# First threshold search of the second MoE layer: next thresholds prepared beside the count, list in three parts, and the second expert's rows turned later

## The chip, the cores and the metric

The kernel runs on one core of a Trainium2 chip. The metric is device time in microseconds (us) of one execution, as a median of several. Engines are named as the profile names them: PE is TensorE (matmuls; PEld its weight loads), DVE is VectorE, ACT is ScalarE, POOL is GpSimd, SP is SyncE, which here issues DMAs. Every engine runs its own instructions strictly in the order in which the program gives them to it; semaphores tie the engines together.

## The reference

Attention over local windows and block summaries gives x of 3072 tokens by 512. A first MoE layer (each token to its best expert) gives a new x. The second MoE layer, where the change is, gives every expert exactly `cap` tokens:

```python
def _moe2_ref(x, w_gate, w1, w2):
    N, D = x.shape; E = w_gate.shape[1]       # 3072, 512, 8
    cap = N // E                              # 384
    logits = x @ w_gate
    order = np.argsort(-logits.flatten())
    assigned = -np.ones(N); counts = np.zeros(E)
    for idx in order:                         # best (token, expert) pair first
        tok, e = idx // E, idx % E
        if assigned[tok] >= 0 or counts[e] >= cap: continue
        assigned[tok] = e; counts[e] += 1
    out = np.zeros((N, D))
    for e in range(E):                        # F = 1024
        mask = assigned == e
        out[mask] = np.maximum(x[mask] @ w1[e], 0.0) @ w2[e]
    return out
```

All data is float32. The results must be near float32, so each operand of a large product is split in two parts, high and low (`wh`, `wl`; `dxh`, `dxl`; `dhh`, `dhl`), and three matmuls stand for one.

## The kernel before

**Stages.** `phase_a` does the attention (to about 178 us), `phase_b` the first experts and the logits of the second layer, left in `Lm` (to about 324 us), `phase_d` the second experts with the routing that `Route2` computes.

**Routing.** The greedy assignment is done in eight phases. Phase `ph` finds the next expert that fills up: a search of NSTEP = 5 steps, each with 31 thresholds, for the logit value at which some expert has `cap` candidates. One step is a chain: thresholds `p_thr` from the step's lower bound (L792, `th` holds the bound `lo`), compares of all tokens' best logits with them (`p_g`, L797), 24 matmuls that count per expert (L806 in phase 0), a comparison with the room that is left (`p_sat`, L816, which also gives the flags `p_any`), a matmul that sums the flags over partitions (L829), and from that the new `lo` (L830). After the search the tokens of this expert are known (`p_t`, L851, summed by matmuls at L859 and L860; positions at L868). `list(ph)` makes a list of their numbers: one-hot matrices `l_A`, `l_bh`, `l_bv` (L888 to L893), matmuls into `dx_ps` (L899, later phases L902), and the index `p_ix` (L909).

**Constants.** `st_ps` is one PSUM tile that holds the small state of the search. `init_state` copies four constants there at the start of phase 0. The reduction into `v` (L778), the first step of a phase, writes to the same tile.

**Experts.** For each expert POOL gathers its 384 rows by three indirect DMAs (L943, tile `xg`), PE transposes them (`xT`, L954, three times four), ACT and DVE split them into `dxh` and `dxl` (L957). L1 is 32 steps of three matmuls (L965, L966, L967), after every fourth of which ACT and DVE make `dhh` (L970) and `dhl` (L972). L2 is 24 steps of three matmuls (L979, L980, L981); after every eighth ACT copies `dz` and POOL scatters it to the output (L986). Weights come by DMA (`wraw`), ACT casts the high part (L927), POOL subtracts for the low part (L936, the function `lows`).

**What sets the order.** From phase 0's list on, a planner in `phase_d` decides while the program is built. It keeps clocks of its own (`now[0]` for PE, `dve`, `pool`), adds an assumed duration for every step that it places, and puts the parts of the next routing phase, the list, the gather, the casts and the transposes between the steps of L1 and L2 as soon as its clock says that they are ready. `xts_step` places the transposes of the next expert at the earliest 4.5 us after the gather by that clock:

```python
if q<=7 and xts.get(q,3)<3 and now[0]>=gath_t[q]+4.5+1.0*xts[q] and (cur is None or npc>=34+4*xts[q]):
```

A change of one of these numbers moves `now[0]`, and with it the place of everything that comes later.

## Time and profile before

| | us |
|---|---|
| median of three runs | 679.68 (677.44 to 681.78) |
| the profiled execution | 682.45 |
| its span in the trace | 680.8 |
| attention and first experts | 0 to 324 |
| search 0, list, gather, transposes | 324.8 to 360.2 |
| second experts, L1 of expert 0 to the last matmul | 360.2 to 675.4 |

The span is the time from the first to the last instruction; 1.65 us of the execution lie outside. A time given in the rows is the distance from the start of the span. In a row of the timeline the brackets at the end say how long the engine was idle before it and what ended that; xN means that N like instructions in a row are taken together. Matmul rows overlap: what counts is the distance of their starts.

### The profile page before, as it was taken

How to read it: one execution, taken by the hardware profiler on the slowest of the kernel's cores; microseconds unless marked ns; L12 is line 12 of the kernel's file. 1: busy time of each engine (PE TensorE's matmuls, PEld its weight loads, DVE VectorE, ACT ScalarE, POOL GpSimd, SP SyncE). 2: the span in 40 equal slices, each digit the busy share in tenths (PEclk: the TensorE clock that was granted, in tenths of full speed). 3: DMA queues.
4: the chain of work that ended last, by engine and by line, in shares of the span. 5: the costliest groups of instructions: out<-in, count | busy, mean ns of one | idle time of the engine just before them, and what ended most of it. 6: DMA issues, size and time to landing. Idle time of an engine off the chain costs nothing.

```text
span 680.8 us, 12765 instructions
## 1 busy us (share of the span) xinstructions
PE 612.7 (90%) x4427; PEld 501.7 (74%) x4427; DVE 487.7 (72%) x1866; ACT 318.4 (47%) x680; POOL 369.6 (54%) x400
## 2 busy tenths in 40 slices
PE   7878975999889999999448999999999999999996
PEld 5667765788567777776327878888897978879895
DVE  5686994889777889683775768788888888862120
ACT  5556873676743856761015135162433526154521
POOL 4322343352146289873027269394876939399841
PEclk8788997899789999998558999999999999999999
DMA  9999899976615987720035072553626154385201
GB/s 239 241 237 240 218 274 192 256 175 200 239 62 187 362 266 224 255 85 23 2 98 197 32 233 79 170 172 123 202 85 209 64 189 153 139 256 182 105 1 46
DMA packets 59778, 114.22 MB, mean 168 GB/s; under 512 B 13537, under 2 KB 23521, under 8 KB 58944
## 3 DMA queue, kind: packets, MB, share of 16 engines
q1 hardware_dynamic: 49968, 79.37, 40.1%
q0 software_dynamic: 9744, 34.02, 15.2%
q8 instruction: 35, 0.57, 0.4%
q14 instruction: 31, 0.25, 0.1%
HBM read 96.54 MB, written 14.88 MB: 164 GB/s over the span
## 4 chain that ended last, share of the span: by engine, by line
PE 22%; issue 10%; POOL 8%; DVE 6%; DMA 4%; ACT 1%; POOLq 0%; DVEq 0%
POOL wl L936 6%; PE dh_ps L965 4%; PE dh_ps L966 4%; PE dh_ps L967 4%; DMA xg<-xrows,p_ix 3%; PE dz_ps L979 2%; PE dz_ps L981 2%; PE dz_ps L980 2%; POOL out_dram L986 1%; PE rt_ps L810 1%; DMA wraw<-in_w1b_dram 1%; DVE p_g L797 1%; PE dh_ps L954 1%; PE rt_ps L806 0%; ACT wh L927 0%
## 5 line engine op out<-in xcount | busy, mean ns | idle before, releaser
L936 POOL TENSOR_TENSOR wl<-wraw,wh 128x512 fp32r<-128x512 f32 x124 | 155.6, 1296 | 5.1 <-ACT wh L927 4.7
L965 PE MATMUL dh_ps<-dxh,wh 128*128 128x384 f32 x256 | 90.0, 351 | 0.7 <-ACT dxh L957 0.7
L927 ACT CAST wh<-wraw 128x512 fp32r<-128x512 f32 x128 | 73.7, 620 | 35.9 <-DMA wraw<-in_w1b_dram 34.1
L966 PE MATMUL dh_ps<-dxl,wh 128*128 128x384 f32 x256 | 87.2, 341 | 0.5 <-DVE dxl L957 0.5
L967 PE MATMUL dh_ps<-dxh,wl 128*128 128x384 f32 x256 | 86.8, 339 | 0.0
L118 POOL TENSOR_TENSOR wraw<-wraw 96x512 f32<-96x512 f32 (+4 forms) x39 | 39.6, 1016 | 80.3 <-DMA wraw<-in_v_dram 77.9
L979 PE MATMUL dz_ps<-wh,dhh 128*128 128x512 f32 x192 | 79.1, 412 | 0.0
L981 PE MATMUL dz_ps<-wh,dhl 128*128 128x512 f32 x192 | 75.9, 395 | 0.0
L980 PE MATMUL dz_ps<-wl,dhh 128*128 128x512 f32 x192 | 75.9, 395 | 0.0
L972 DVE SCALAR_TENSOR_TENSOR dhl<-dh_ps,dhh 128x384 fp32r<-128x384 f32 x64 | 35.1, 555 | 49.0 <-ACT dhh L970 48.6
L986 POOL DMA_INDIRECT out_dram<-dz,io x24 | 24.3, 1014 | 81.3 <-ACT dz L984 78.5
L970 ACT ACTIVATE dhh<-dh_ps 128x384 fp32r<-128x384 f32 x64 | 31.4, 491 | 75.3 <-PE dh_ps L967 75.3
L984 ACT COPY dz<-dz_ps 128x512 f32<-128x512 f32 x24 | 14.1, 586 | 102.8 <-PE dz_ps L981 56.8
L138 ACT ACTIVATE p_e<-s_sb,nm 128x118 f32<-128x118 f32 x192 | 59.7, 385 | 0.9 <-DVE nm L132 0.9
L504 POOL TENSOR_TENSOR wl<-wraw,wh 128x1024 fp32r<-128x1024 f32 (+1 forms) x18 | 38.1, 2144 | 28.3 <-ACT wh L503 28.3
L503 ACT CAST wh<-wraw 128x1024 fp32r<-128x1024 f32 (+1 forms) x56 | 48.9, 932 | 8.0 <-DMA wraw<-in_w1a_dram 6.1
L943 POOL DMA_INDIRECT xg<-xrows,p_ix x24 | 23.4, 974 | 52.2 <-DVE rrow L875 32.5
L128 PE MATMUL s_ps<-kt,Q 128*128 128x118 f32 x192 | 42.5, 306 | 9.3 <-DVE kt L108 6.7
L965 PEld LDWEIGHTS dh_ps<-dxh,wh 128*128 128x128 f32 x256 | 48.8, 190 | 1.5 <-ACT dxh L957 0.9
L966 PEld LDWEIGHTS dh_ps<-dxl,wh 128*128 128x128 f32 x256 | 48.7, 190 | 1.3 <-DVE dxl L957 1.1
L967 PEld LDWEIGHTS dh_ps<-dxh,wl 128*128 128x128 f32 x256 | 48.7, 190 | 0.0
L504 DVE TENSOR_TENSOR wl<-wraw,wh 128x1024 fp32r<-128x1024 f32 (+1 forms) x38 | 42.7, 1163 | 8.0 <-ACT wh L503 8.0
(355 smaller groups left out, 1476.9 us busy)
## 6 DMA issues: line engine op xcount, KB each, us to landing
wraw<-in_w1b_dram SPq DMA_DIRECT2D x15, 1024.0 KB
wraw<-in_w2b_dram POOLq DMA_DIRECT2D x14, 1024.0 KB, 7.4
wraw<-in_w2a_dram SPq DMA_DIRECT2D x12, 1024.0 KB
wraw<-in_w1a_dram SPq DMA_DIRECT2D x10, 1024.0 KB
VV<-in_v_dram SPq DMA_DIRECT2D x16, 585.0 KB
kt<-in_k_dram SPq DMA_DIRECT2D x16, 412.0 KB
qd<-in_q_dram SPq DMA_DIRECT2D x16, 384.0 KB
wraw<-in_v_dram SPq DMA_DIRECT2D x8, 768.0 KB
```

The source lines that it names most:

```text
L128: T.matmul(p[:,j,0:118],d['q2'][:,h,w,:],d['k2'][:,h,w//2,:] if w%2 else d['kt'][:,h,64*w:64*w+118],start=True,stop=True)
L138: A.activation(pe[:,j,:],sb[:,j,:],AF.Exp,bias=nm[:,j:j+1],scale=-1.0)
L503: (hi.tensor_copy if hi else nc.scalar.copy)(h[:,c],t[:,c])
L504: (lo or nc.vector).tensor_tensor(l[:,c],t[:,c],h[:,c].bitcast(F32),op=OP.subtract)
L927: A.copy(h[:,c],t[:,c])
L936: eng.tensor_tensor(l[:,c],t[:,c],h[:,c].bitcast(F32),op=OP.subtract)
L965: T.matmul(q,wh[:,c],s['xh'][:,d,:],start=(d==0),stop=False)
L966: T.matmul(q,wh[:,c],s['xl'][:,d,:],start=False,stop=False)
L967: T.matmul(q,wl[:,c],s['xh'][:,d,:],start=False,stop=(d==3))
L979: T.matmul(q,s['hh'][:,f,c0],wh[:,c],start=(f==0),stop=False)
L980: T.matmul(q,s['hh'][:,f,c0],wl[:,c],start=False,stop=False)
L981: T.matmul(q,s['hl'][:,f,c0],wh[:,c],start=False,stop=(f==7))
```

## The change

1. `init_state` copies the four constants with ACT, all at the start of phase 0; before, DVE did two ahead of L778 and two in step 0, behind the compares. The addition that completes `Lm` is moved behind the two instructions that make `pm`.
2. In phase 0, the thresholds of steps 1 to 4 are made from the count directly: `pre` (the threshold numbers times the next width, plus the old lower bound) is computed after `p_sat`, and one SCALAR_TENSOR_TENSOR adds the count times the width. The new `lo` is computed behind the compares. The count's matmul writes `dx_ps` instead of `rt_ps`.
3. In phase 0's list, `l_A` is laid out with the weights of a matmul contiguous, is written last, and in three parts.
4. In the planner, the transposes of expert 1 are placed at the earliest 6.0 us after its gather by the planner's clock; 4.5 for the others as before.

```diff
--- before.py
+++ after.py
@@ -723,10 +723,10 @@
         for j in range(4): WC[k,j]=W.split(RAW[j],G if j==3 else None)
         xT(k); L1(k,0); L1(k,1); hT(k); L2(k); yT(k); place(k,pfc,cfc); direct(k); put(k)
         G.indirect_dma_start(out=xr,out_offset=bass.IndirectOffsetOnAxis(ap=gcol[:,1:2],axis=0),in_=YR[k],in_offset=None,bounds_check=128+N-1,oob_is_err=False)
-    Lm=st['Lm'].rearrange("p e c->p (e c)"); V.tensor_tensor(Lm,Lm,lgp[:,0:192],op=OP.add)
 
     V.tensor_reduce(st['pm'],st['pmx'],AX.X,OP.max)
     V.tensor_scalar(st['pm'].bitcast(U32),st['pm'].bitcast(U32),0x7F800000,None,op0=OP.bitwise_and)
+    Lm=st['Lm'].rearrange("p e c->p (e c)"); V.tensor_tensor(Lm,Lm,lgp[:,0:192],op=OP.add)
 
 NSTEP=5; J=31; BIG=1e30
 
@@ -752,11 +752,8 @@
     def state(self,nm,dt=None):
         return self.q[nm].bitcast(dt) if dt else self.q[nm]
     def init_state(self):
-        V=self.nc.vector; st=self.st
-        for nm,src in (('c8',st['c8']),('jr',self.jr)): V.tensor_copy(self.q[nm],src)
-        yield
-        for nm,src in (('colid',st['colid']),('p0',self.p0)): V.tensor_copy(self.q[nm],src)
-        yield
+        A=self.nc.scalar; st=self.st
+        for nm,src in (('c8',st['c8']),('jr',self.jr),('colid',st['colid']),('p0',self.p0)): A.copy(self.q[nm],src)
     def wide(self,ph): return 2 if ph<3 else 4
     def psum(self):
         return self.ps.tile([128,512],F32,name="rt_ps",bufs=1)
@@ -773,8 +770,8 @@
 
         nc,st,wk=self.nc,self.st,self.wk; V=nc.vector; T=nc.tensor
         B3=[128,8,24]; B4=[128,2,8,24]; Lm=self.Lm; c8=st['c8']
-        ini=self.init() if ph==0 else iter(()); inq=self.init_state() if ph==0 else iter(()); Q=self.state
-        next(inq,None)
+        ini=self.init() if ph==0 else iter(()); Q=self.state
+        if ph==0: self.init_state()
         v=Q('v'); V.tensor_reduce(v,Lm.rearrange("p e c->p c e"),AX.X,OP.max)
         if ph: yield 0.4,0
         cand=wk.tile(B3,BF,name="p_cand"); V.tensor_tensor(cand,Lm,v[:,None,:].to_broadcast(B3),op=OP.is_ge)
@@ -789,13 +786,17 @@
         if ph<7:
             low=self.nM
             for s in range(NSTEP):
-                thr=wk.tile([128,32],F32,name="p_thr"); V.tensor_scalar(thr,Q('jr'),ws[:,s:s+1],low,op0=OP.mult,op1=OP.add)
+                thr=wk.tile([128,32],F32,name="p_thr")
+
+
+                if ph==0 and s: V.scalar_tensor_tensor(thr,p[:,0:1].to_broadcast([128,32]),ws[:,s-1:s],pre,op0=OP.mult,op1=OP.add)
+                else: V.tensor_scalar(thr,Q('jr'),ws[:,s:s+1],low,op0=OP.mult,op1=OP.add)
                 if s==0: yield 1.3,0
                 g=wk.tile([128,24,32],BF,name="p_g")
                 for c0,c1 in (((0,12),(12,20),(20,24)) if ph==0 else ((0,24),)):
                     B=[128,c1-c0,32]
                     V.tensor_tensor(g[:,c0:c1],v[:,c0:c1,None].to_broadcast(B),thr[:,None,:].to_broadcast(B),op=OP.is_ge)
-                if s==0: next(inq,None)
+                if ph==0 and s: V.tensor_scalar(lo,p[:,0:1],ws[:,s-1:s],low,op0=OP.mult,op1=OP.add); low=lo
                 nw=self.wide(ph) if ph>=1 else 1
                 yield ((2.3+0.2*nw if ph>=2 else 1.4) if s else 1.1),(0.7 if ph<1 else 0.8/self.wide(ph))
                 p=self.psum()
@@ -814,6 +815,7 @@
                 if ph==0:
                     sat=wk.tile([J,8],BF,name="p_sat")
                     V.tensor_scalar(sat,p[0:J,0:8],0.0,0.0,op0=OP.is_ge,op1=OP.max,accum_out=anys)
+                    if s<NSTEP-1: pre=wk.tile([128,32],F32,name="p_pre"); V.tensor_scalar(pre,Q('jr'),ws[:,s+1:s+2],low,op0=OP.mult,op1=OP.add)
                 else:
                     R=32; sat=wk.tile([32,8],F32,name="p_sat1"); e=wk.tile([32,1],F32,name="p_e")
                     V.tensor_tensor_reduce(out=sat,in0=p[0:R,0:8],in1=self.r[0:R] if ph<1 else d[0:R],scale=1.0,scalar=-1e9,op0=OP.subtract,op1=OP.max,accum_out=e)
@@ -826,8 +828,8 @@
                 else:
                     if ph: V.tensor_scalar(anys,e[0:J],0.0,None,op0=OP.is_ge)
                     yield (0.7 if ph else 0.35),0.05
-                    p=self.psum(); T.matmul(p[:,0:1],st['ones_b'][0:J,:],anys,start=True,stop=True)
-                V.tensor_scalar(lo,p[:,0:1],ws[:,s:s+1],low,op0=OP.mult,op1=OP.add); low=lo
+                    p=self.psum() if ph else self.ps.tile([128,512],F32,name="dx_ps",bufs=1); T.matmul(p[:,0:1],st['ones_b'][0:J,:],anys,start=True,stop=True)
+                if ph or s==NSTEP-1: V.tensor_scalar(lo,p[:,0:1],ws[:,s:s+1],low,op0=OP.mult,op1=OP.add); low=lo
             V.tensor_scalar(hi,lo,ws[:,NSTEP-1:NSTEP],None,op0=OP.add)
         else:
             for x in (lo,hi): V.tensor_copy(x,self.nM)
@@ -886,17 +888,21 @@
         if ph: yield 0.7,0
         A=wk.tile([128,32,24],BF,name="l_A"); bh=wk.tile([128,12,24],BF,name="l_bh"); bv=wk.tile([128,2,12,24],BF,name="l_bv")
         V.tensor_tensor(bh,st['it32'][:,0:12],bf[:,None,:].to_broadcast([128,12,24]),op=OP.is_equal)
-        if n<4: V.tensor_tensor(A,st['it32'],sf[:,None,:].to_broadcast([128,32,24]),op=OP.is_equal)
+        if ph==0: A=A.rearrange("p s c->p (s c)").rearrange("p (c s)->p c s",c=24)
+        elif n<4: V.tensor_tensor(A,st['it32'],sf[:,None,:].to_broadcast([128,32,24]),op=OP.is_equal)
         else: A=A.rearrange("p s c->p (s c)").rearrange("p (c s)->p c s",c=24); V.tensor_tensor(A,st['it_b'][:,None,0:32].to_broadcast([128,24,32]),sf[:,:,None].to_broadcast([128,24,32]),op=OP.is_equal)
         if ph: yield 0.9,0
         V.tensor_tensor(bv[:,0],bh,self.state('p0')[:,:,None].to_broadcast([128,12,24]),op=OP.mult)
         V.tensor_tensor(bv[:,1],bh,self.state('colid')[:,None,:].to_broadcast([128,12,24]),op=OP.mult)
+        if ph==0:
+
+            for c0,c1 in ((0,12),(12,20),(20,24)): B=[128,c1-c0,32]; V.tensor_tensor(A[:,c0:c1],st['it_b'][:,None,0:32].to_broadcast(B),sf[:,c0:c1,None].to_broadcast(B),op=OP.is_equal)
         yield (0.6 if n<4 else 1.0),(0.65 if n<4 else 0.25)
         o=self.ps.tile([128,512],F32,name="dx_ps",bufs=1)
         oc=wk.tile([128,2,12],F32,name="l_oc"); o1=self.state('oc')[0:32]
         if n<4:
             o=o[0:32,0:24]
-            for c in range(24): T.matmul(o,A[:,:,c],bv[:,:,:,c],start=(c==0),stop=(c==23))
+            for c in range(24): T.matmul(o,A[:,:,c] if ph else A[:,c],bv[:,:,:,c],start=(c==0),stop=(c==23))
             o=o.rearrange("p (v b)->p v b",v=2); V.tensor_copy(oc[0:32,0],o[:,0]); V.tensor_copy(o1,o[:,1])
         else:
             for c in range(0,24,n): T.matmul(o[:,0:96],A[:,c:c+n].rearrange("p c s->p (c s)"),bv[:,:,:,c:c+n].rearrange("p v b c->p c v b"),start=(c==0),stop=(c==24-n))
@@ -1047,7 +1053,7 @@
         return conv_step(q,(0,0,18,34) if cur is not None else (0,0,0,0))
     def xts_step():
         q=curp+1
-        if q<=7 and xts.get(q,3)<3 and now[0]>=gath_t[q]+4.5+1.0*xts[q] and (cur is None or npc>=34+4*xts[q]):
+        if q<=7 and xts.get(q,3)<3 and now[0]>=gath_t[q]+(6.0 if q==1 else 4.5)+1.0*xts[q] and (cur is None or npc>=34+4*xts[q]):
             xT(q,xts[q]); xts[q]+=1; now[0]+=0.45; return True
         return False
     hk=True; HOLD=3.0
```

DVE at the end of expert 0, between its search's second and third count of phase 2, before and after (`p_g` are compares, `dxl` the low part of expert 1's rows, of which there are three, `p_d` the take-up of a count):

```order
L797 TENSOR_TENSOR p_g<-st_ps,p_thr 128x768
L957 TENSOR_TENSOR dxl<-dh_ps,dxh 128x4x128
L813 TENSOR_TENSOR p_d<-rrow,rt_ps 32x8
L819 ISA p_sat_5541,p_e<-rt_ps,p_d 32x8
L819 ISA p_e 32x1
L823 TENSOR_SCALAR p_an_5544<-p_e 32x1 x4
L824 STREAM_TRANSPOSE p_tr<-p_an_5544 128x32
L825 TENSOR_REDUCE p_cnt<-p_tr 128x1
L830 TENSOR_SCALAR th<-p_cnt,ws,th 128x1
L792 TENSOR_SCALAR p_thr<-st_ps,ws,th 128x32
L797 TENSOR_TENSOR p_g<-st_ps,p_thr 128x768
L957 TENSOR_TENSOR dxl<-dh_ps,dxh 128x4x128 x2
```

```order
L798 TENSOR_TENSOR p_g<-st_ps,p_thr 128x768
L814 TENSOR_TENSOR p_d<-rrow,rt_ps 32x8
L821 ISA p_sat_5545,p_e<-rt_ps,p_d 32x8
L821 ISA p_e 32x1
L825 TENSOR_SCALAR p_an_5548<-p_e 32x1 x4
L826 STREAM_TRANSPOSE p_tr<-p_an_5548 128x32
L827 TENSOR_REDUCE p_cnt<-p_tr 128x1
L832 TENSOR_SCALAR th<-p_cnt,ws,th 128x1
L793 TENSOR_SCALAR p_thr<-st_ps,ws,th 128x32
L798 TENSOR_TENSOR p_g<-st_ps,p_thr 128x768
L963 TENSOR_TENSOR dxl<-dh_ps,dxh 128x4x128 x3
L814 TENSOR_TENSOR p_d<-rrow,rt_ps 32x8
```

The first `dxl` has moved from ahead of the second take-up to behind the third compare, where it stands with the other two. Line numbers shift: L957 is L963, L797 is L798. On PE the transposes have moved with it. Behind the list came three steps of L2, a count, four steps, transposes, a count, transposes, one step, transposes, two steps, a count and L1. Now it is three steps, a count, five steps, a count, one step, two sets of transposes, one step, the third set, one step of L1, a count, and the rest of L1.

PE in expert 2, from the last matmul of `p_t` on to the first of L2, before and after (each three rows `dh_ps` are one step of L1):

```order
L860 MATMUL rt_ps<-p_t_6368,ones_b 128x1
L965 MATMUL dh_ps<-dxh,wh 128x384
L966 MATMUL dh_ps<-dxl,wh 128x384
L967 MATMUL dh_ps<-dxh,wl 128x384
L965 MATMUL dh_ps<-dxh,wh 128x384
L966 MATMUL dh_ps<-dxl,wh 128x384
L967 MATMUL dh_ps<-dxh,wl 128x384
L965 MATMUL dh_ps<-dxh,wh 128x384
L966 MATMUL dh_ps<-dxl,wh 128x384
L967 MATMUL dh_ps<-dxh,wl 128x384
L979 MATMUL dz_ps<-wh,dhh 128x512
```

```order
L862 MATMUL rt_ps<-p_t_6381,ones_b 128x1
L971 MATMUL dh_ps<-dxh,wh 128x384
L972 MATMUL dh_ps<-dxl,wh 128x384
L973 MATMUL dh_ps<-dxh,wl 128x384
L971 MATMUL dh_ps<-dxh,wh 128x384
L972 MATMUL dh_ps<-dxl,wh 128x384
L973 MATMUL dh_ps<-dxh,wl 128x384
L985 MATMUL dz_ps<-wh,dhh 128x512
```

Three steps of L1 stand behind `p_t` before, two after; the same holds at experts 3 to 5. Ahead of the list's matmuls then come nine steps of L2 before and ten after. Behind the list, the first transposes of the next expert come after eight steps of L2 before and after seven, the second after nine and eight, the third then with no step of L2 between but one count of the search. In search 0 itself the order on DVE is that of the diff.

POOL between expert 6 and expert 7 (`wl` are weight differences of expert 6, `xg` the gather of expert 7, `in_w2b_dram` its weights), before and after:

```order
L986 DMA out_dram<-dz,io 3072x512
L936 TENSOR_TENSOR wl<-wraw,wh 128x512 x3
L943 DMA xg<-xrows,p_ix_8247 128x516 x3
L946 TENSOR_SCALAR io<-p_ix_8247 128x3
L936 TENSOR_TENSOR wl<-wraw,wh 128x512 x9
```

```order
L992 DMA out_dram<-dz,io 3072x512
L942 TENSOR_TENSOR wl<-wraw,wh 128x512 x11
L949 DMA xg<-xrows,p_ix_8271 128x516 x3
L952 TENSOR_SCALAR io<-p_ix_8271 128x3
L955 TENSOR_LOAD p_ei_8143
L955 ISA x2
L521 ISA
L521 DMA wraw<-in_w2b_dram 128x4x512
L521 ISA
```

The gather of expert 7 has moved behind eight more differences, and two weight loads have come to POOL, which SP issued before.

## Rows read from the trace of the kernel before

**Rows 1.** The page, part 1: busy us, share of the span, instructions.

```profile
PE 612.7 (90%) x4427; PEld 501.7 (74%) x4427; DVE 487.7 (72%) x1866; ACT 318.4 (47%) x680; POOL 369.6 (54%) x400
```

**Rows 2.** Timeline, VectorE, head of the search (columns: start us, us, engine).

```profile
324.81 0.35 DVE L726 TENSOR_TENSOR Lm<-Lm,lgp 128x192 f32<-128x192 f32 x1 [2.61 <-PEq L712]
...
325.77 0.62 DVE L778 TENSOR_REDUCE st_ps<-Lm 128x24 f32<-128x192 f32 x1
...
327.40 0.29 DVE L767 TENSOR_REDUCE i_a<-rt_ps 128x1 f32<-128x128 f32 x1 [0.23 <-PE rt_ps L766]
```

**Rows 3.** Groups of ACT over the whole span: busy us, mean ns, idle before.

```profile
L664 ACT ACTIVATE e_d<-e_d 128x24 f32<-128x24 f32 x1 | 0.2, 223 | 2.7 <-DVE r_cand L338 2.7
```

**Rows 4.** Timeline, all engines, one step of the search.

```profile
330.98 0.31 DVE L792 TENSOR_SCALAR p_thr<-st_ps,ws,th 128x32 f32<-128x32 f32 x1
...
331.94 0.82 PE L806 MATMUL rt_ps<-p_oh,p_g 128*31 128x8 bf16 x24 [0.78 <-DVE p_g L797]
...
332.80 0.15 DVE L816 TENSOR_SCALAR_CACHE_REDUCE p_sat<-rt_ps 31x8 bf16<-31x8 f32 x1 [0.38 <-PE rt_ps L806]
...
333.21 0.28 DVE L830 TENSOR_SCALAR th<-rt_ps,ws,th 128x1 f32<-128x1 f32 x1 [0.25 <-PE rt_ps L829]
333.53 0.31 DVE L792 TENSOR_SCALAR p_thr<-st_ps,ws,th 128x32 f32<-128x32 f32 x1
```

**Rows 5.** Line L863: xcount, duration ns min/median/max.

```profile
L863 DVE SCALAR_TENSOR_TENSOR st_ps<-p_x,st_ps x8: 186/186/189, 345.8 to 599.0; 128x24 f32<-128x24 f32 x8
```

**Rows 6.** Timeline, all engines, list of the first expert.

```profile
347.90 0.95 DVE L889 TENSOR_TENSOR l_A<-it,st_ps 128x768 bf16<-128x768 bf16 x1
...
349.13 0.45 DVE L893 TENSOR_TENSOR l_bv<-l_bh,st_ps 128x288 bf16<-128x288 bf16 x1
349.63 1.77 PE L899 MATMUL dx_ps<-l_bv,l_A 128*32 128x24 bf16 x24 [4.39 <-DVE l_bv L893]
```

**Rows 7.** Timeline, all engines, gather and first transposes.

```profile
352.63 1.01 POOL L943 DMA_INDIRECT xg<-xrows,p_ix  x1 [32.48 <-DVE rrow L875]
...
356.11 0.66 PE L954 MATMUL dh_ps<-cb,xg 128*128 128x128 f32 x4 [0.49 <-DMA xg<-xrows,p_ix]
```

**Rows 8.** Windows: us, busy us of five engines, granted clock, DMA share, GB/s.

```profile
360.85:364.26 3.41, 3.37 (x11) 3.37 (x11) 0.85 (x1) 1.08 (x3) 0.38 (x1) 0.50 1.01 359
```

**Rows 9.** Tile p_ix, all 24 gathers of the second experts.

```profile
DMA to landing us min/median/max: 3.6/4.6/5.6
```

**Rows 10.** Timeline, all engines, end of expert 0 and start of expert 1.

```profile
403.99 0.66 PE L954 MATMUL dh_ps<-cb,xg 128*128 128x128 f32 x4 [1.18 <-DMA xg<-xrows,p_ix]
...
404.57 0.56 PE L810 MATMUL rt_ps<-p_oh,p_g 128*64 128x16 bf16 x12
...
405.30 0.69 DVE L957 TENSOR_TENSOR dxl<-dh_ps,dxh 128x512 fp32r<-128x512 f32 x1 [2.34 <-ACT dxh L957]
...
409.19 0.57 PE L810 MATMUL rt_ps<-p_oh,p_g 128*64 128x16 bf16 x12 [0.93 <-DVE p_g L797]
...
410.38 0.44 PE L966 MATMUL dh_ps<-dxl,wh 128*128 128x384 f32 x1 [0.26 <-DVE dxl L957]
```

**Rows 11.** Timeline, all engines, expert 3 with the list of expert 4.

```profile
507.89 0.56 DVE L972 SCALAR_TENSOR_TENSOR dhl<-dh_ps,dhh 128x384 fp32r<-128x384 f32 x1 [0.48 <-ACT dhh L970]
...
513.50 1.17 PE L902 MATMUL dx_ps<-l_bv,l_A 128*128 128x96 bf16 x6
...
514.88 0.18 DVE L904 COPY l_oc<-dx_ps 32x24 f32<-32x24 f32 x1
...
523.16 0.66 PE L954 MATMUL dh_ps<-cb,xg 128*128 128x128 f32 x4 [0.39 <-DMA xg<-xrows,p_ix]
```

**Rows 12.** Line L979 from 507.0 to 513.45 us: xcount, ns, first and last start.

```profile
L979 PE MATMUL dz_ps<-wh,dhh x9: 392/394/400, 507.2 to 512.8; 128*128 128x512 f32 x9
```

**Rows 13.** Timeline, GpSimd and TensorE, ahead of expert 7.

```profile
610.02 3.80 POOL L936 TENSOR_TENSOR wl<-wraw,wh 128x512 fp32r<-128x512 f32 x3
...
625.09 0.60 PE L954 MATMUL dh_ps<-cb,xg 128*128 128x128 f32 x4
```

## What the change will do: the prediction

> **What bounds the kernel now.** The page comes first: TensorE is busy 90% of the span, VectorE 72%, GpSimd 54% [rows 1]. An average says little about a change in one stage, so the timeline of each stage follows. It shows two regimes. From 324.8 us to 360.2 us, between the two MoE layers, TensorE has almost nothing to do: a serial chain runs through VectorE (thresholds, compares), TensorE (counts), VectorE again, the list, GpSimd's gather and the transposes [rows 2, 4, 6, 7]. What leaves this chain leaves the time, one for one. From 360.2 us TensorE works almost without a pause to the end. There a move costs nothing as long as its operand is there when TensorE reaches it, and the reader is to look at TensorE's idle time ahead of an instruction: 1.18 us at the first transposes of expert 1, 0.93 and 0.26 us behind them [rows 10], 0.39 us at the third transposes of expert 4 [rows 11]. The change touches both regimes: the chain by its code, the rest by one number of the planner, which gives another order for experts 1 to 7.
>
> **Head of the search, constants on ACT: +0.3 us.** Two copies leave VectorE ahead of the reduction into v, which started at 325.77 [rows 2]. In their place stand four ACT copies. Built, the first waits for the Lm addition, and the reduction at L778 waits for the fourth, since all four write st_ps. With pm first, the Lm addition (0.35 us, the next start 0.28 behind its own) ends near 325.4. No row shows this copy; the nearest is a small ACT instruction of 24 columns, 0.223 us [rows 3]. Four of them take 0.9 us, so the reduction starts at 326.3, 0.55 us late. Of that, 0.23 us is covered: so long VectorE waits for pm's matmul at L767 [rows 2]. I take +0.3. Bounds: 0 (copies so short or so far overlapped that the cover holds) and +0.55 (no cover). The two copies that leave step 0 lay beside TensorE's counts, for which VectorE waits 0.38 us in a step [rows 4]; they give nothing.
> [...]
>
> **Search steps: -1.06 us.** A step takes 333.53 - 330.98 = 2.55 us, five in a row. Behind the flags (332.80 + 0.15) VectorE waits 0.25 us for their count, makes `lo` (L830, 333.21), and only then the thresholds (L792, 333.53, 0.31 us) [rows 4]. After the change `pre` is computed in that wait, and one STT makes the thresholds from the count. `pre` starts near 332.98, takes the 0.31 us of the L792 row and ends at 333.29, 0.08 after the count was there. The STT has no row of this shape; the nearest of 24 columns took 0.19 us [rows 5], the TENSOR_SCALAR of the same 32 columns 0.31 [rows 4]. With 0.25 it runs from 333.32 to 333.57, where the old thresholds ended at 333.84: 0.26 us, in four steps 1.06. Bounds 0.8 and 1.3. The `lo` that is moved behind the compares lies in VectorE's 0.38 us wait, so it costs nothing; the last step keeps its `lo` on the path.
>
> **List in three parts: -0.85 us.** L889 to L893 keep VectorE busy until 349.58, and 24 matmuls of the list run from 349.63 for 1.77 us, 70 ns apart [rows 6]. Two things change. TensorE may start when the first of three parts of A is written: A now stands last, and its first 12 columns, half of the 0.95 us of L889, are needed; the other half, less what three instructions cost more than one, leaves the way: 0.26 us. And the weights lie contiguous. The counts of a step also have contiguous weights and need 0.82 us for 24 matmuls, 27 ns apart [rows 4], but stream 8 columns where the list streams 24 strided ones. The later lists stream 96 strided columns per matmul, six in 1.17 us [rows 11], about 0.17 us each by their starts, or 1.75 ns per column: 42 ns for 24. At 42 ns the list ends 24 x 28 ns = 0.67 us sooner, with the start, rounded down, 0.85. Bounds: 0.26 (the strided stream sets the 70 ns) and 1.2 (27 ns, held by the third part of A).
> [...]
>
> So expert 0 starts 0.3 - 1.06 - 0.85 = -1.6 us, sooner. Gather and first matmuls hang on this chain without slack: issue at 352.63, transposes at 356.11 with TensorE waiting for the rows [rows 7].
>
> **Boundary of expert 0 to 1: -0.8 us.** The planner now turns the rows of expert 1 later, behind nine L2 steps instead of seven, and puts the third count behind the first L1 step. TensorE was ready for the rows at 402.81 and waited 1.18 us [rows 10]; two L2 steps fill that wait (0.705 us each: 507.17 to 512.80 for eight of them [rows 12]). The second count comes at 403.5 instead of 404.57. From it to the third one, which waited for its compare, it was 4.6 us, 0.8 of that one dxl in between (0.69 us and the turn), which now stands behind: the compare ends near 407.3, three dxl near 409.3. So L966 starts between 409.1 and 409.3 instead of 410.38, with one count (0.5 us) to come that before was done. Net 0.8 at the earlier end; bounds 0.3 and 1.2.
>
> **Boundaries 1 to 2 up to 5 to 6: +1.9 us.** In the old order three L1 steps stand behind p_t and nine L2 steps ahead of the list; in the new one two and ten (at expert 1 two and nine, now none and ten). p_t's own move costs nothing: VectorE stands 0.48 us at L972, waiting for the last L1 part, before it goes on with the list [rows 11]. But the list's matmuls come one L2 step, 0.705 us, later on TensorE. Their result was there at 514.67 + 0.04, and VectorE took it at 514.88: 0.17 us of slack. So p_ix, the gather and its rows come 0.53 us later. The third transposes already wait for these rows, 0.39 us [rows 11], so TensorE loses the 0.53. The pattern stands three times (lists at 474.70, 513.50 and 552.47, each with 0.21 us from the last matmul's end to L904): 1.6 us. At the lists of 435 us and 592 us the same reading leaves more slack; I put 0.3 on the two together. Bounds: 0 (the new position of the transposes hides it) and 0.705 x 4 = 2.8.
>
> **Expert 7: +1.7 us.** In the old order GpSimd runs 3 weight differences (1.27 us each) from 610.02 [rows 13], then the gather of expert 7, then 9 more. In the new one 11 stand ahead: 610.02 + 11 x 1.27 = 624.0, and then the gather. Queued behind it on GpSimd are the io offsets, a register load, and now the two loads of w2b that SP issued. Rows need 3.48 us from issue to the transposes [rows 7]: 627.5. TensorE comes there one L2 step after the old 625.09 [rows 13], at 625.8. It stands 1.7 us and has no pause later in which to win it back. Bounds: 0 (the differences run sooner, and the gather with them) and 2.5 (rows of 4.3 us). The two loads come some 5 us later; their weights are used 30 us after that.
>
> **The sum.** -1.6 - 0.8 + 1.9 + 1.7 = +1.2 us. On the profiled execution, 682.45 us, that is 683.65; on the median of the three runs, 679.68, which the profiled one exceeds by 2.8, it is **680.9 us**. A difference of 1%, 6.8 us, is about what a measurement of this kernel can tell from none; this is well inside.
>
> **Rivals.** (a) The moves are hidden, only chain and first boundary show: list and gather have slack that one execution doesn't show, and expert 7's rows come in time. Then -2.4 us, 677.3. For it: the waits in question are 0.2 to 0.4 us long. Against: TensorE waits for the DMA at exactly those transposes. (b) Slower, through the rows: the gather is last at every boundary. If the slack of 0.17 us is none and expert 7's rows take 5.6 us to land, the longest landing that the tile view of p_ix has [rows 9], the boundaries cost 2.8 and expert 7 (624.0 + 5.6 - 625.8) 3.8 us: -2.4 + 2.8 + 3.8 = +4.2, 683.9. It decides against the forecast once expert 7's rows land after 628. [...] (d) The change doesn't do what it says: if `pre` and the STT cost as much as `lo` and the thresholds did, the steps give 0, and it is 682.0.
>
> **How the numbers follow.** Forecast 0.45, (a) 0.27, (b) 0.13, (c) 0.1, (d) 0.05. The forecast's own bounds, half of each added, are 678.5 to 683; (a) with the clock reaches down to 675.6, (b) up to 683.9, and three runs of the old kernel lie 4.3 us apart. The range is 675.5 to 684.5. Beyond 1%: faster (below 672.9) 0.04, where chain, boundary and clock all take their best bound; slower (above 686.5) 0.05, (b) with a second slow stretch.
>
> **What would show it.** In the new trace: the v reduction about 0.5 us later behind four ACT copies; steps of 2.29 us; list matmuls 40 ns apart; the first gather near 351.0 us; no wait for rows at expert 1; 0.8 to 0.9 us of waiting at the third transposes of experts 3 to 5; 1.7 us at the first of expert 7. If the waits at experts 3 to 7 are as small as before, the planner's part is free and (a) holds; if the steps still take 2.55 us, (d).

## The result, and the profile after

The changed kernel took **687.19 us** (median of 6 runs, 682.43 to 688.60) against 678.49 of the kernel before beside it: ratio **1.0105 [1.0071, 1.0139]**, slower, and outside the predicted range. Timed again later, in 12 runs beside 22 of before, the same kernel stood at 1.0044 [1.0007, 1.0082]. Both are slower, by less than 2%; how much of that is the change itself is taken up further down. In all comparisons, runs that lie over 1.5% above the fastest of their kernel are left out.

The profiled execution took 688.28 us, 5.8 more than that of before, for a span of 686.6. The page, part 1, of the kernel after:

```profile
PE 612.8 (89%) x4424; PEld 502.6 (73%) x4427; DVE 486.3 (71%) x1868; ACT 318.9 (46%) x684; POOL 368.9 (54%) x402
```

No engine is busy over 1 us longer [rows 1]: what was added is waiting, and stretches in which the clock granted to TensorE was 0.50. I count from the first instruction of the search on VectorE, at 324.81 us before and at 322.82 after; what lies ahead is the same code. The timeline of the chain after (columns as in [rows 2]):

```profile
323.47 0.17 ACT L756 COPY st_ps<-cb 128x8 f32<-128x8 f32 x1 [4.66 <-DVE Lm L729]
...
324.11 0.16 ACT L756 COPY st_ps<-cc 128x1 f32<-128x1 f32 x1
...
324.30 0.62 DVE L775 TENSOR_REDUCE st_ps<-Lm 128x24 f32<-128x192 f32 x1 [0.86 <-ACT st_ps L756]
...
328.55 0.30 DVE L818 TENSOR_SCALAR p_pre<-st_ps,ws,nM 128x32 f32<-128x32 f32 x1
...
328.95 0.25 DVE L792 SCALAR_TENSOR_TENSOR p_thr<-dx_ps,ws,p_pre 128x32 f32<-128x32 f32 x1
...
331.20 0.25 DVE L792 SCALAR_TENSOR_TENSOR p_thr<-dx_ps,ws,p_pre 128x32 f32<-128x32 f32 x1
...
346.36 1.24 PE L905 MATMUL dx_ps<-l_bv,l_A 128*32 128x24 bf16 x24 [4.11 <-DVE l_A L899]
...
348.83 1.00 POOL L949 DMA_INDIRECT xg<-xrows,p_ix  x1 [29.41 <-DVE rrow L877]
```

VectorE waits 0.86 us for the four copies, a step takes 331.20 - 328.95 = 2.25 us instead of 2.55 [rows 4], the list's 24 matmuls 1.24 us instead of 1.77 [rows 6]. The gather starts 348.83 - 322.82 = 26.01 us behind the head, before 27.82 [rows 7]: the chain is 1.81 us shorter, as designed. The timeline from expert 0 to expert 4 after, where TensorE waits:

```profile
356.54 0.45 PE L971 MATMUL dh_ps<-dxh,wh 128*128 128x384 f32 x1 [0.68 <-ACT dxh L963]
...
360.43 2.18 ACT L933 CAST wh<-wraw 128x512 fp32r<-128x512 f32 x4 [3.95 <-DMA wraw<-in_w1b_dram]
...
362.52 0.48 ACT L976 ACTIVATE dhh<-dh_ps 128x384 fp32r<-128x384 f32 x1
363.03 0.56 DVE L978 SCALAR_TENSOR_TENSOR dhl<-dh_ps,dhh 128x384 fp32r<-128x384 f32 x1 [4.96 <-ACT dhh L976]
...
364.21 0.17 PE L831 MATMUL rt_ps<-p_any,ones_b 31*128 31x1 bf16 x1 [2.46 <-DVE p_any L829]
...
407.96 0.44 PE L971 MATMUL dh_ps<-dxh,wh 128*128 128x384 f32 x1 [1.24 <-ACT dxh L963]
...
408.81 0.44 PE L972 MATMUL dh_ps<-dxl,wh 128*128 128x384 f32 x1 [0.41 <-DVE dxl L963]
...
429.79 0.16 PE L861 MATMUL rt_ps<-p_t,tri_b 128*128 128x2 bf16 x1 [0.30 <-DVE rrow L858]
...
445.14 0.66 PE L960 MATMUL dh_ps<-cb,xg 128*128 128x128 f32 x4 [0.75 <-DMA xg<-xrows,p_ix]
...
526.37 0.66 PE L960 MATMUL dh_ps<-cb,xg 128*128 128x128 f32 x4 [0.48 <-DMA xg<-xrows,p_ix]
```

Expert 0 starts 33.72 us behind the head, before 35.35. Then TensorE stands 2.46 us at a count of the next search: the flags (L829) are queued on VectorE behind `dhl` (L978), `dhl` waits for `dhh` on ACT, and that stands behind four casts which waited for the second weight chunk to land. The rows of expert 1 are in time, as forecast, but TensorE waits 1.24 and 0.41 us for their high and low parts; expert 2's rows are late by 0.75 us. The windows view after, of the two stretches at half clock (granted 0.50) in experts 0 and 1 (columns as in [rows 8]):

```profile
365.17:372.00 6.83, 6.83 (x32) 5.91 (x31) 3.33 (x10) 3.00 (x6) 5.68 (x5) 0.50 0.00 2
...
409.54:412.96 3.42, 3.42 (x21) 3.39 (x19) 2.58 (x12) 0.00 (x0) 3.22 (x5) 0.50 0.70 276
```

They follow the waits of 2.46 and of 1.24 + 0.41 us. Before had one there, of 3.41 us [rows 8]. In them L1's matmuls start 320 ns apart, after as before (medians); outside them, in the same experts, 177 ns after and 174 before. The loss is counted here and further on as half of a stretch, an estimate from the granted 0.50: 5.12 us here against 1.71. From the distances it is 0.45 of a stretch, 4.6 against 1.6 us. At expert 7, GpSimd and TensorE in the timeline after:

```profile
613.74 13.76 POOL L942 TENSOR_TENSOR wl<-wraw,wh 128x512 fp32r<-128x512 f32 x11
...
627.66 0.99 POOL L949 DMA_INDIRECT xg<-xrows,p_ix  x1 [0.16 <-issue]
...
631.19 0.63 PE L960 MATMUL dh_ps<-cb,xg 128*128 128x128 f32 x4 [1.00 <-DMA xg<-xrows,p_ix]
```

Eleven weight differences, then the gather, as forecast. Taken from the head, the pair of profiles differs so: -1.64 to the start of expert 0, +3.50 in its L1 (wait and clock), +1.97 to the start of expert 2 (1.71 of it clock), +1.23 to that of expert 6, +2.69 to the last matmul: +7.75 us.

### The profile page after: what moved, and what is told of

It is laid out like the page before. It is cut to its first block, busy times and chain, and to the rows that moved or that the text cites. A ratio compares the mean times of both kernels' runs of the same rounds, so it can differ in the third digit from the quotient of the medians.

```text
span 686.6 us, 12779 instructions
## 1 busy us (share of the span) xinstructions
PE 612.8 (89%) x4424; PEld 502.6 (73%) x4427; DVE 486.3 (71%) x1868; ACT 318.9 (46%) x684; POOL 368.9 (54%) x402
## 3 DMA queue, kind: packets, MB, share of 16 engines
q0 software_dynamic: 10288, 36.12, 16.1%
## 4 chain that ended last, share of the span: by engine, by line
POOL 17%; issue 16%; PE 10%; DVE 4%; DMA 4%; ACT 1%; POOLq 1%; DVEq 0%; ACTq 0%
POOL wl L942 13%; POOL out_dram L992 3%; PE dh_ps L971 2%; PE dh_ps L972 2%; PE dh_ps L973 2%; DMA xg<-xrows,p_ix 2%; DMA wraw<-in_w2b_dram 1%; DMA wraw<-in_w1b_dram 1%; PE dz_ps L985 1%; PE dz_ps L987 1%; PE dz_ps L986 1%; POOL xg L949 1%; POOL wraw L521 1%; PE rt_ps L807 1%; PE rt_ps L811 1%
## 5 line engine op out<-in xcount | busy, mean ns | idle before, releaser
L971 PE MATMUL dh_ps<-dxh,wh 128*128 128x384 f32 x256 | 91.7, 358 | 1.9 <-ACT dxh L963 1.9
L972 PE MATMUL dh_ps<-dxl,wh 128*128 128x384 f32 x256 | 88.4, 345 | 0.7 <-DVE dxl L963 0.7
L978 DVE SCALAR_TENSOR_TENSOR dhl<-dh_ps,dhh 128x384 fp32r<-128x384 f32 x64 | 34.8, 553 | 50.1 <-ACT dhh L976 49.8
L504 DVE TENSOR_TENSOR wl<-wraw,wh 128x1024 fp32r<-128x1024 f32 (+1 forms) x38 | 44.9, 1219 | 9.0 <-ACT wh L503 8.9
L972 PEld LDWEIGHTS dh_ps<-dxl,wh 128*128 128x128 f32 x256 | 49.4, 193 | 1.4 <-DVE dxl L963 1.2
```

Of the source, the lines that this page charges most:

```text
L504: (lo or nc.vector).tensor_tensor(l[:,c],t[:,c],h[:,c].bitcast(F32),op=OP.subtract)
L971: T.matmul(q,wh[:,c],s['xh'][:,d,:],start=(d==0),stop=False)
L972: T.matmul(q,wh[:,c],s['xl'][:,d,:],start=False,stop=False)
```

## The experiments

Three theories. **A**: the loss lies in the planner's order of experts 1 to 7. **B**: it lies in the shorter chain, which brings TensorE early to the flags' wait and so to the half clock. **F**: it is the late gather of expert 7. The change has four parts: C the chain's code, T the later turn of expert 1, O the order of lists and rows of experts 2 to 7, G the late gather. Differences are of means, in us, to the runs of before that were taken beside the kernel; the ratio is another measure and need not agree with them to 1 us (turn_alone). Theories C to F in the expectations are not the parts.

| kernel | parts | runs | ratio [95%] | difference |
|---|---|---|---|---|
| changed kernel | C T O G | 6 | 1.0105 [1.0071, 1.0139] | +7.8 |
| after_again | C T O G | 12 | 1.0044 [1.0007, 1.0082] | +3.2 |
| warm_wait | C T O G | 6 | 1.0115 [1.0062, 1.0168] | +6.7 |
| after_two_sp | C T O G | 10 | 1.0024 [0.9983, 1.0065] | +2.2 |
| plan_only | T O G | 12 | 1.0095 [1.0061, 1.0130] | +5.8 |
| plan_again | T O G | 11 | 1.0035 [0.9999, 1.0071] | +2.4 |
| gather7_early | C T O | 12 | 1.0029 [0.9996, 1.0062] | +2.1 |
| plan_g7 | T O | 12 | 1.0016 [0.9978, 1.0054] | +1.5 |
| turn625 | C T | 12 | 1.0028 [1.0000, 1.0057] | +2.3 |
| t_first | C T | 10 | 1.0016 [0.9979, 1.0052] | +1.0 |
| turn_warm | C T | 12 | 1.0014 [0.9978, 1.0050] | +0.7 |
| turn_alone | T | 12 | 1.0001 [0.9970, 1.0032] | +1.0 |
| late37 | C O G | 12 | 0.9996 [0.9963, 1.0029] | +0.1 |
| late37_g7 | C O | 12 | 1.0010 [0.9976, 1.0044] | +0.8 |
| late37_alone | O G | 11 | 1.0035 [0.9997, 1.0073] | +2.7 |
| chain_only | C | 12 | 0.9976 [0.9944, 1.0008] | -1.4 |
| relu_first | C | 11 | 1.0004 [0.9969, 1.0039] | +0.2 |
| two_sp | C | 12 | 0.9960 [0.9927, 0.9992] | -2.5 |

**The number alone, and the chain alone.** plan_only (and later plan_again) is before with the new number:

```diff
-now[0]>=gath_t[q]+4.5+1.0*xts[q]
+now[0]>=gath_t[q]+(6.0 if q==1 else 4.5)+1.0*xts[q]
```

> The kernel before with one number of the planner changed (expert 1's transposes at 6.0 instead of 4.5), so experts 1 to 7 run in the order of the changed kernel, and the search and first list are as before. Theory A (the loss lies in the order of experts 1 to 7): 6 to 9 us slower than before. Theory B (about half the loss is made in expert 0, where the shorter chain meets weights that don't land sooner and the clock falls): 4 to 6 us slower. The prediction's terms for the order alone gave +2.8 us. If it is within 2 us of before, both theories fall.

chain_only is the changed kernel with the edit reversed.

```diff
-now[0]>=gath_t[q]+(6.0 if q==1 else 4.5)+1.0*xts[q]
+now[0]>=gath_t[q]+4.5+1.0*xts[q]
```

> The changed kernel with the planner's number put back to 4.5, so only the head, the search and the list of phase 0 are changed and the order of experts 0 to 7 is that of before. Theory A: 1.6 us faster than before, as the prediction's chain terms say. Theory B: L1 of expert 0 starts 1.6 us sooner, TensorE waits about 2.5 us at the first flags' matmul of the next search (behind casts that wait for the second weight load), and the end is 1 to 3 us slower than before.

The number alone is slower by 5.8 us, which lies just under what A asked for and within what B allowed. The chain alone decides: -1.4 us, where A said -1.6 and B +1 to +3. A holds. warm_wait tries B a second time: it keeps TensorE busy with idle matmuls in the flags' wait:

```diff
+if ph==1 and s==0: warm(nc,st,self.ps.tile([128,512],F32,name="dz_ps",bufs=2),11)
 p=self.psum() if ph else self.ps.tile([128,512],F32,name="dx_ps",bufs=1); T.matmul(p[:,0:1],st['ones_b'][0:J,:],anys,start=True,stop=True)
```

> The changed kernel with 11 idle matmuls (no use of their result) put on TensorE ahead of the first flags' matmul of phase 1, where it waited 2.46 us in the profile of after. If the fall of the clock in expert 0 (granted 0.50 from 365.17 to 372.00) comes from that wait: no such stretch there, L1 of expert 0 some 3.4 us shorter, the time 3 us under that of after. If the clock falls for another reason, the same stretch is there and the time is that of after within 1 us.

Its profile has no half clock in any expert, but it is of the fastest of the six runs (680.20 us). The granted clock of all six over the whole span says more: 0.945 on average, 0.944 in the runs of before beside them, and yet 6.7 us slower. The clock alone is not the cause.

**The late gather.** gather7_early, plan_g7 and late37_g7 put it ahead of expert 6's weight differences:

```diff
+if q==7 and q not in gath_t and q in listed: gather(q); gath_t[q]=max(pool[0],now[0]); pool[0]=gath_t[q]+3.1; xts[q]=0; return True
 if curp>=0 and cur is not None and conv_step(curp,(0,0,0,0)): return True
```

> The changed kernel with expert 7's gather put ahead of expert 6's weight differences on GpSimd as soon as its list is there (and with it the w2b loads back on SP). The prediction's term for expert 7 (the rows come late): no wait at the first transposes of expert 7 (it was 1.0 us), the time 1 to 2 us under that of after. If that wait was covered otherwise: same as after.

It stands 5.7 us under the changed kernel's first measurement and 1.1 us under its second; 1 to 2 was expected. In its timeline the gather starts some 13 us sooner behind the head than in the kernel after, and TensorE does not wait at expert 7:

```profile
610.42 0.99 POOL L949 DMA_INDIRECT xg<-xrows,p_ix  x1 [0.16 <-issue]
```

**Expert 1's turn alone.** turn625 keeps the later turn and gives experts 2 to 7 their old order:

```diff
-gath_t[q]+(6.0 if q==1 else 4.5)
+gath_t[q]+(6.25 if q==1 else 4.5)
```

> The changed kernel with 6.25 in place of 6.0 in the planner. Expert 1's rows are still turned later (behind nine L2 steps), but the planner falls back into the old order from the middle of expert 1 on: two L1 steps behind p_t and nine L2 steps ahead of the list, expert 7's gather ahead of the weight differences. Theory C (the loss lies in the order of experts 2 to 7, not in the later turn of expert 1): 0.5 to 1 us faster than the chain alone, so 2 to 3 us faster than before, and 8 us faster than the changed kernel. Theory D (the later turn itself costs, through the waits and the clock at the start of expert 1): 1 to 3 us slower than the chain alone, about as before or slower.

It is 2.3 us slower than before and 3.7 us slower than the chain alone: D, the later turn itself costs.

t_first adds to it, and relu_first to chain_only, an ACT order in which expert 0's first `dhh` stands ahead of the casts of the second chunk:

```diff
-if curp>=0 and cur is not None and conv_step(curp,(0,0,0,0)): return True
+if curp>=0 and cur is not None and conv_step(curp,(0,5 if curp==0 else 0,0,0)): return True
...
-return conv_step(q,(0,0,18,34) if cur is not None else (0,0,0,0))
+return conv_step(q,(0,0,18,34) if cur is not None else (0,99 if q==0 else 0,0,0))
...
-if xts.get(q,0)==3 and conved.get(q,0)>=8:
+if xts.get(q,0)==3 and conved.get(q,0)>=(8 if q else 4):
```

> The kernel with 6.25 and one more change: ACT's first relu of expert 0 stands ahead of the four casts of the second weight chunk instead of behind them (the order of the other engines is the same). If the chain's gain is lost in expert 0 because TensorE waits for flags that stand behind a cast that waits for weights: no wait of 2.5 us at the first flags' matmul of phase 1, L1 of expert 0 ends about 1.2 us sooner after the head of the search, and the time is 1 us under that with 6.25 alone. If the weights bind L1 of expert 0 in any case (its second half needs the second chunk): same end of L1, same time.

> The chain alone (planner's number 4.5) with ACT's first relu of expert 0 ahead of the casts of the second weight chunk. As for the other: with the lost gain given back, 1 us faster than the chain alone, so 2.5 us faster than before; otherwise as the chain alone.

Neither differs from its base by more than the intervals, and neither base has the flags' wait in its own profile, so what that wait costs where it stands stays open. turn_warm fills the wait ahead of expert 1's L1 in turn625 with idle matmuls:

```diff
+if q==1: warm(nc,st,ps.tile([128,512],F32,name="dz_ps",bufs=2),8)
```

> The kernel with 6.25 and 8 idle matmuls on TensorE ahead of L1 of expert 1, where it waited 1.97 us. If that wait brings the fall of the clock in expert 1 (granted 0.50 for 6 us in the profile with 6.25, for 3.4 us in two others with the later turn, never with the old turn): no such stretch, and the time 1 to 2 us under that with 6.25. If not: the same time.

Its time is not resolved from turn625 either. Its profile has no half clock in expert 1, but t_first and copies_dve have the same 1.97 us wait unfilled and none there either, so the wait does not bring the fall each time. copies_dve (one profile, not timed) is turn625 with the four copies on VectorE as before (the calls that step `init_state` come back with them):

```diff
-A=self.nc.scalar; st=self.st
-for nm,src in (('c8',st['c8']),('jr',self.jr),('colid',st['colid']),('p0',self.p0)): A.copy(self.q[nm],src)
+V=self.nc.vector; st=self.st
+for nm,src in (('c8',st['c8']),('jr',self.jr)): V.tensor_copy(self.q[nm],src)
+yield
+for nm,src in (('colid',st['colid']),('p0',self.p0)): V.tensor_copy(self.q[nm],src)
+yield
```

> The kernel with 6.25 and the four constant copies back on DVE, two ahead of the reduction and two behind the first compares. One look, for the head: with ACT the reduction into v began 1.48 us after the first instruction of the head and the first thresholds 3.83 us after it. The prediction's term (0.3 us lost by ACT): the first thresholds come 0.2 to 0.3 us sooner. Its bound of 0: the same.

Its first thresholds start 3.59 us behind the head, turn625's 3.84: the move to ACT costs 0.25 us in this pair.

**Without the later turn.** late37 leaves expert 1 as before and gives experts 3 to 7 the new order and the late gather; late37_g7 has the early one.

```diff
-gath_t[q]+(6.0 if q==1 else 4.5)
+gath_t[q]+(5.5 if q==2 else 4.5)
```

> The changed kernel's code with expert 1's rows turned as before (4.5) and 5.5 for expert 2 alone. The boundary 0 to 1 has the old order, experts 3 to 7 the new one: two L1 steps behind p_t, ten L2 steps ahead of the list, expert 7's gather behind 11 weight differences. The boundary 1 to 2 gets an order that neither kernel has (its rows turned after ten L2 steps). Theory E (what the traces add up: 3 us for the order of experts 2 to 7, the chain's gain nearly gone by the end of L1 of expert 0, the later turn of expert 1 worth nothing): 2 to 3 us slower than before. Theory F (the order of the late experts is worth what the timed runs say, 5 us and more): 4 us or more slower. The clock stretch in expert 1 shouldn't come.

> late37 with expert 7's gather ahead of expert 6's weight differences. Prediction's term for expert 7: 1.7 us under late37 (traces so far: 1.5). Timed comparison of the earlier pair: 4 to 5 us under it. Between the two the interval should tell: at 3 us or more the late gather costs more in most runs than in the profiled ones.

Neither is slower than before beyond its interval, and the gather makes no difference that the intervals resolve: F falls, the 2 to 3 us of E are missed too, and it looked as if the parts did not add up. two_sp is chain_only with expert 0's second weight chunk loaded by SP right behind the first:

```diff
-range(4 if 'x' in S.get(p,()) else 1 if p==0 else 2)
+range(4 if 'x' in S.get(p,()) else 2 if p==0 else 2)
```

> The chain alone with the second weight chunk of expert 0 loaded by SP right behind the first instead of by GpSimd behind the gather. If the chain's gain is lost because expert 0's weights land too late: ACT's casts of the second chunk some 5 us sooner, no wait behind them, L1 of expert 0 ends 1 us or more sooner after the head, and the time is 1 to 3 us under before. If L1 of expert 0 is bound by the search on DVE anyway: same end of L1, and the time of the chain alone.

It is the one kernel whose interval lies below before, by 0.4%; against chain_only, -1.0 +- 1.2 us, nothing is resolved. In its timeline ACT's casts of the second chunk wait for no weights and start 34.83 us behind the head, 2.9 sooner than in chain_only:

```profile
355.23 0.66 PE L960 MATMUL dh_ps<-cb,xg 128*128 128x128 f32 x4 [2.05 <-DMA xg<-xrows,p_ix]
...
356.40 2.18 ACT L933 CAST wh<-wraw 128x512 fp32r<-128x512 f32 x4
```

But the third rows are late by 2.05 us, and the last matmul of expert 0's L1 starts 59.2 us behind the head, 59.1 in chain_only. That the sooner weights gave the time is not shown.

**Do the parts add up?** Three kernels have parts on before's chain (turn_alone with 6.25, late37_alone with 5.5 at expert 2, plan_g7), after_two_sp is the changed kernel with two_sp's edit, and the two kernels with the whole order were timed again, unchanged.

> The kernel before with the value 6.0 at expert 1 (its later turn and the new order of experts 2 to 7), but expert 7's gather ahead of expert 6's weight differences. If the parts add up (turn +3, lists and rows of 2 to 7 +1.3, gather +1.7 us): +4.3 us against the kernel before, ratio 1.006. If the late gather costs 5 us beside the later turn: +0.4, ratio 1.001, 5 us below the kernel with the value alone (1.0095).

> The kernel before with 6.25 at expert 1: its rows are turned later, experts 2 to 7 keep the old order, the chain is the old one. By the prediction's term for this boundary -0.5 us, ratio 0.999. If the turn costs 3 us, as the three kernels with it and the new chain suggest (1.002 on average, over a chain worth 1.8 us): +3, 1.0045.

> The kernel before with 5.5 at expert 2: old turn at expert 1, new order for experts 3 to 7 with the late gather of expert 7, old chain. By the traces of the same order with the new chain +2.7 us, ratio 1.004; if parts add up as the timed runs have it (0.9996 with a chain worth 1.8 us): +1.8, 1.0027. If lists and gather are free without the later turn: 1.000.

> The changed kernel, with the second weight chunk of expert 0 loaded by SP right behind the first. If the parts add up (+6 for the order, -2.5 for chain and load): +3.5 us, ratio 1.005, with the first six runs of the changed kernel above their mean. If the late gather costs more beside the later turn: +6.5 to +7, ratio 1.010.

> The changed kernel itself, timed beside the next one. If the parts add up (chain -1.8, order of experts 1 to 7 with the late gather +4 to +5 us): ratio 1.003 to 1.005. If the late gather costs more beside the later turn, as the first measurement has it: 1.010.

> The kernel before with the value 6.0 at expert 1 alone, beside the changed kernel on one chip: the difference of the two is what the chain gives. If the chain's gain lasts: 1.8 us above the changed kernel, ratio 1.006 to 1.008. If it is lost beside the later turn, as the two first measurements have it (1.0105 and 1.0095): the same as the changed kernel, within 1 us.

Roughly. late37_alone, after_two_sp and after_again came out as expected for a sum or below it, turn_alone between its two values, plan_g7 (+1.5 us) nearer to the 0.4 of the other case. Fitted as a sum of four parts and weighted by their errors, the 18 differences give C -0.8, T +1.9, O +0.6, G +1.5: **+3.3 us** for the whole. They scatter 1.6 times as far as the runs of a kernel do, so each part is known to 0.5 to 1.0 us. The first measurements of the changed kernel, of warm_wait and of plan_only lie 4.4, 3.4 and 1.7 us above the sum; without these three the whole is +2.4.

That no part costs more beside another is not shown. A term for C and T together takes +1.6 +- 1.1 us, one for T and G +1.4 +- 1.4. And plan_again, which should stand 1.8 us above after_again if the chain's gain lasts, stood 0.9 +- 1.0 below: beside the later turn no gain of the chain is seen. The 20 profiles are a second account: from the head to the last matmul, without the clock's loss, they give C +0.1, T +1.3, O +1.9, G +1.2, each +- 0.4 to 0.5, so +4.4.

The changed kernel's two profiles lie 7.9 us apart, 4.0 of it ahead of the search, in code that the change leaves alone. Of the 3.8 behind its head the clock is 3.4: after_again has one stretch in experts 0 and 1, and a shorter wait at the flags. Its windows view and its timeline:

```profile
354.19:357.60 3.41, 3.41 (x13) 3.38 (x11) 0.27 (x1) 0.97 (x2) 0.27 (x1) 0.50 0.97 350
```

```profile
360.40 0.17 PE L831 MATMUL rt_ps<-p_any,ones_b 31*128 31x1 bf16 x1 [0.74 <-DVE p_any L829]
```

The 20 profiles of the kernels lose 0 to 5.9 us by such stretches, with the old turn (up to 5.1 in late37_g7) as with the new, and with either chain.

## Why the prediction was wrong

The forecast was +1.2 us; the parts as timed make +3.3. Two steps failed: that the chain's 1.6 us reach the end (0.8 +- 0.5 timed), and the boundary of expert 0 to 1 (-0.8 forecast, +1.9 +- 0.6 timed). With them put right the sum is 683.0 us, within the range, as is the second measurement, 682.37. What lifts the first to 687.19 is in no part; see the rivals.

**The chain: its length right, its gain not kept.** Head +0.20 us (first thresholds 3.83 behind the head, before 3.63; predicted +0.3), steps 4 x 0.30 = -1.2 (-1.06), the list the rest of the 1.81: -0.8 (-0.85), its matmuls 45 ns apart by their starts (42). The head's cover, VectorE's wait of 0.23 us at L767 in [rows 2], stands in two of six profiles with the old chain; in the four others the first thresholds come at 3.31, and against these the new head is 0.5 longer. What failed is the step to the total, that what leaves the chain leaves the time, one for one: over 14 profiles with the new chain and 6 with the old one, L1 of expert 0 starts 1.2 us sooner and ends 0.7 sooner. In each of the 14, one of two things meets the shorter chain: the third rows land late (TensorE waits 1.45 us or more, as in chain_only below), or TensorE waits 0.74 to 2.67 us at the flags, behind casts that wait for the second weight chunk (in warm_wait idle matmuls fill that wait). The chain moves neither. Why the rows land late in some executions was not shown.

A second reason stands in the distance of L1's matmuls, here by their line in L1 of expert 7, 32 of them: plan_only, with the old chain, and the kernel after.

```profile
L965 PE MATMUL dh_ps<-dxh,wh x32: 336/336/339, 640.9 to 657.0; 128*128 128x384 f32 x32
```

```profile
L971 PE MATMUL dh_ps<-dxh,wh x32: 337/338/342, 647.2 to 663.7; 128*128 128x384 f32 x32
```

Three matmuls follow each other between two of these, so they stand 16.1 / 93 = 173 and 16.5 / 93 = 177 ns apart. The last section tells at which experts, and what it comes to.

**Boundary of expert 0 to 1: the step that failed.** -0.8 was predicted, the timed turn costs +1.9 +- 0.6. The term filled the 1.18 us wait of [rows 10]. That wait does not stand in every execution: of seven profiles with the old turn four have it (1.22, 1.18, 0.54, 0.41 us), three do not. chain_only's timeline, third transposes of expert 0, first of expert 1, and the waits behind them:

```profile
354.80 0.66 PE L960 MATMUL dh_ps<-cb,xg 128*128 128x128 f32 x4 [1.88 <-DMA xg<-xrows,p_ix]
...
398.82 0.66 PE L960 MATMUL dh_ps<-cb,xg 128*128 128x128 f32 x4
...
404.02 0.57 PE L811 MATMUL rt_ps<-p_oh,p_g 128*64 128x16 bf16 x12 [0.92 <-DVE p_g L798]
...
405.21 0.45 PE L972 MATMUL dh_ps<-dxl,wh 128*128 128x384 f32 x1 [0.26 <-DVE dxl L963]
```

And the new turn, in plan_again's:

```profile
404.70 0.45 PE L965 MATMUL dh_ps<-dxh,wh 128*128 128x384 f32 x1 [1.25 <-ACT dxh L957]
...
405.55 0.44 PE L966 MATMUL dh_ps<-dxl,wh 128*128 128x384 f32 x1 [0.41 <-DVE dxl L957]
```

These two waits, 1.7 us together, stand in all eight profiles with 6.0: the transposes now lie right ahead of L1, and TensorE waits for their high and low parts. With the old turn the two waits behind the transposes make 0.6 to 1.2 us, and the rows' wait comes to that only in some executions.

From the end of expert 0's L1 to the second matmul of expert 1's (L966, after L972), without the clock's loss, the old turn takes 24.2 to 25.6 us, the profile of before at the upper end, mean 24.74; the new one 24.1 to 24.2. That gain is 0.6 on average, and 1.4 only against the profile of before. Behind it the term counted 0.5 us for the count that is still to come, and that alone uses up the 0.6. From the second matmul on to the start of expert 2 the new turn takes 41.4 us, the old one 40.0 (means of 8 and 7): the count, the wait of 0.30 us for p_t (429.79 after), and the rows of expert 2, 0 to 0.75 us late (445.14); the prediction had put 0.3 us on the lists at 435 and 592 us together. So the traces show a loss of 0.8 to 0.9 us where 0.8 was to be won; the 1 us more that the timed runs have is within twice its error, and where it lies was not found. 6.25 instead of 6.0 moves the same loss ahead: 25.4 and 40.0.

**Boundaries up to 6: the size right by the traces, the mechanism in part.** The waits at the third transposes of experts 3 to 5 are 0.59, 0.48 and 0.60 us after, where 0.8 to 0.9 was predicted; over all profiles they grew by 0.05 to 0.2 us, not by the 0.53 that the term moved into them, and the second transposes wait 0.1 to 0.2 more. From the start of expert 2 to that of expert 6 the new order takes 0.8 us more on the new chain and 1.0 more on the old. From there to the start of expert 7 it takes 0.9 more with the early gather too, without a wait: six matmuls of a list have moved there from ahead of expert 6. Together +1.8 by the profiles, predicted 1.9, timed +0.6 +- 0.9. The waits that the traces show between experts 2 and 6 account for 0.8 of the 1.8; the rest was not traced.

**Expert 7: right by the profiles.** Late against early gather costs 1.3 to 1.5 us from expert 6 to the end, timed +1.5 +- 1.0; predicted +1.7. The wait is 1.0 to 1.5 us in seven profiles with the late gather and none in the eighth, warm_wait's, where TensorE had waited 1.55 us for rows of expert 6 just before.

**The rivals.** (d) falls with the step of 2.25 us, (a) with the wait at expert 7, (b) with the gathers' landing: 3.4 to 3.7 us in the profile after, none 5.6. (c) is the chance of TensorE's clock, which the range's lower end, 675.6, holds at 1.7 us. No run shows that term as a time of its own; it is half of the 3.41 us at the granted clock 0.50 [rows 8]. By the same estimate the profile after lost 3.4 us more than that of before: the right thing, at too small a size. Of the 8.7 us between the first medians 3.3 are the sum of the parts, which the terms should have given; the clock's stretches account for some of the rest. The six first runs of the changed kernel have a mean granted clock of 0.940, the twelve later ones 0.948, and their means lie 3.7 us apart; within the kernels a clock lower by 0.001 goes with 0.28 us, which makes an estimate of 2.2 us. What remains was not settled: plan_only's profile has a single stretch, and its runs still lay 5.8 us above before, 2.4 when timed again. The 0.05 that was given to a time above 686.5 rested on (b) with a second stretch; the stretch came, (b) did not.

## What to carry to other kernels

A wait seen in one profile is a draw: before a term is built on filling it, see whether it stands in other executions, or put in both cases. When one number of a planner shifts the work of all later stages, price each boundary from the operands of the first moved instruction to the start of the next stage, and not just the wait that is to go. A shorter serial chain gives time only up to the next thing that it does not move, here, by TensorE's waits in the traces, the landing of rows or of weights.

## What the runs showed of the hardware that was not expected

L1's matmuls take one of two spacings per expert, 173 to 174 or 175 to 177 ns (medians of an expert, outside the stretches at half clock), always the same in builds of one chain: the six profiles with the old code have the longer one at experts 2 and 5, the fourteen with the new one at 0, 1, 3, 4, 6 and 7. Four experts more by 96 x 3 to 4 ns are 1.2 to 1.5 us, most of the 1.8 that the chain is shorter. It repeats with period three, and there are three weight buffers; copies_dve has it too, so the ACT copies are not its cause. Whether it comes from where the buffers lie was not tried.

The same gather of expert 0 lands its third rows so that L1 starts 33.7 to 35.3 us behind the head with one chain code, a spread as large as the whole chain's gain. Two measurements of one kernel, each with an interval of +-0.35%, came out 0.6% apart: a difference below 1% wants a second measurement here.
